# A recurrent cross-attention block with a maxout FFN: the state folded into the first layer, and the batches interleaved by hand

## The chip, the cores and the metric

The kernel runs on one core of one Trainium2 chip. A core has TensorE (PE) for matmuls, VectorE (DVE), ScalarE (ACT) and GpSimd (POOL) for elementwise work, and SyncE (SP), which here only issues transfers. Matmuls read SBUF and write PSUM, which has 8 banks of 2 KB for each of 128 partitions; DVE and ACT read PSUM. Each engine runs its own instructions in order and waits on semaphores for the others. The metric is the device time of one execution in microseconds (us).

## What is computed

There are B = 8 batches and H = 8 heads, S = 512 tokens and Ns = 32 state rows in each, D = 64 columns a head. Tokens read the state and the state reads the tokens, both by softmax attention; the heads are put side by side (8 x 64 = 512 columns), which gives 8 x (512 + 32) = 4352 rows; each row then passes a layer that takes the maximum of three products, and an output layer.

```python
def _attn_ref(x, state):
    scores = scale * np.matmul(x, state.transpose(0, 1, 3, 2))
    ...
    xread = np.matmul(a, state)
    scores2 = scale * np.matmul(state, x.transpose(0, 1, 3, 2))
    ...
    sread = np.matmul(a2, x)
    return np.concatenate([xread, sread], axis=2)

def _moe_ref(x, w1, w2, w3, w_out):
    h = np.maximum(np.maximum(x @ w1, x @ w2), x @ w3)
    return h @ w_out
```

`a` and `a2` are the softmaxes of the two score matrices. d_model is 512 and d_ff is 768. The kernel takes and gives float32 and computes in bfloat16 with float32 sums.

## The kernel before

The program has four stages, written one after the other; the Tile framework's scheduler sets the order of each engine's instructions within what the data and the buffers allow, so the end of one stage mixes with the start of the next.

*Loads.* POOL issues every load, since a transfer that converts float32 to bfloat16 is issued there: the state twice (L65, and L73 eight times into the block-diagonal `bd_sb`), x in 32 pieces (L85: one for each batch and each 128 tokens, 128 bytes a run in SBUF), then the weights w1, w2, w3 (L90) and w_out (L93).

*State.* 32 small transposes and 64 small ACT copies build `stateT_bd` (L96 to L110), the transposed state with two heads on the diagonal.

*Attention,* for each batch and each 128 tokens (L125 to L176): four transposes of x (`pxt`, helper L48) and an ACT copy `xT`; four 64-column matmuls `ps` (L143) for the scores; the exponential `e_b` on ACT (L151); row sums `den`, reciprocals `rden` and the product `a_sb` on DVE (L157 to L162); two transposes `pat` and a DVE copy `aT_b` (L176). Then for each pair of heads (L178 to L219) a 64-row matmul `pxr` (L184) multiplies a by the state, and ACT copies it into `AT` (L191); eight small matmuls `psr` (L195, L203) and three DVE operations give the state's own reads, also into `AT`.

*FFN* over `AT`, 4352 columns in nine tiles of 512 (the last has 256): for each of six blocks `m` of d_ff, three groups of four matmuls `pw` (L240) with K = 512 in four steps; ACT copies the first (L249) and DVE takes two maxima (L250, L251) into `ht`. Then for each 128 tokens six matmuls `po` (L256), an ACT copy (L264) and a transfer to HBM on SP (L265).

Of the kernel before, what the change touches and what calls it, by code (L numbers as in the profile page):

```python
# [8 lines left out]
F32 = mybir.dt.float32  # L10
BF16 = mybir.dt.bfloat16
AX = mybir.AxisListType
AF = mybir.ActivationFunctionType


@with_exitstack
def kernel(
# [9 lines left out]
):  # L27
    nc = tc.nc
# [5 lines left out]
    T = B * SP  # L34
    d_model, d_ff = moe_w1.shape
    assert HD == d_model
    assert out.shape[0] == T and out.shape[1] == d_model

    NSC = S // 128
    NKT = HD // 128  # L40
    NMT = d_ff // 128
    NKO = d_ff // 128
    NHP = H // 2

    scale = 1.0 / (D ** 0.5)

    def tr(out_ap, in_ap, ident_ap, *, start, stop, tile_position=(0, 0)):
        nc.tensor.matmul(out_ap, in_ap, ident_ap,  # L48
                         is_transpose=True, start=start, stop=stop,
                         tile_position=tile_position)  # L50

    const = ctx.enter_context(tc.tile_pool(name="const", bufs=1))
    ident = const.tile([128, 128], BF16)
    make_identity(nc, ident)
    ones128 = const.tile([128, 128], BF16)
    nc.gpsimd.memset(ones128, 1.0)

    inpool = ctx.enter_context(tc.tile_pool(name="in", bufs=1))
    atpool = ctx.enter_context(tc.tile_pool(name="at", bufs=1))
    wpool = ctx.enter_context(tc.tile_pool(name="weights", bufs=1))  # L60

    AT = atpool.tile([128, NKT, T], BF16)

    state_sb = inpool.tile([32, B, H, D], BF16)
    nc.gpsimd.dma_start(out=state_sb, in_=state.rearrange("b h n d -> n b h d"))  # L65

    bd_sb = inpool.tile([128, B, 2, 128], BF16)
    nc.gpsimd.memset(bd_sb, 0.0)
    for hq in range(2):
        for hp4 in range(4):  # L70
            h = hq * 4 + hp4
            c0 = (h % 2) * 64
            nc.gpsimd.dma_start(  # L73
                out=bd_sb[hp4 * 32:(hp4 + 1) * 32, :, hq, c0:c0 + 64],
                in_=state[:, h, :, :].rearrange("b n d -> n b d"),
            )

    stateT_bd = inpool.tile([128, B, NHP, 2 * Ns], BF16)
    nc.gpsimd.memset(stateT_bd, 0.0)

    x_sb = inpool.tile([128, B, NSC, H, D], BF16)
    xr = x.rearrange("b h (sc p) d -> p b sc h d", p=128)
    for b in range(B):
        for sc in range(NSC):
            nc.gpsimd.dma_start(out=x_sb[:, b, sc, :, :], in_=xr[:, b, sc, :, :])  # L85
# [211 lines left out]
```

## Time and profile before

| | |
|---|---|
| runs | 279.34, 281.24, 280.69 us; median 280.69 |
| span of the profiled execution, first to last instruction | 279.6 us (its own device time is not listed apart from the runs) |
| mean granted TensorE clock | 0.896 |
| loads: read from HBM | 15.73 MB |
| results: written to HBM | 8.91 MB |
| FFN stage without gaps on PE | from 101 us on |

A line of the profile's groups names the source line, the engine, the operation, what is written and read, the shape and the count; then the busy time in us, the mean of one in ns, and the time that the engine stood idle just before them with what ended it. In the chain of waits each piece is the work that released the next. The page cuts the span into 40 slices; a digit is a share in tenths, and PEclk is the clock that TensorE was granted. A piece of the timeline merges neighbouring instructions of one kind; matmuls overlap, so the time of a piece is the pitch from start to start times the count less one, and the whole duration of the last.

### The profile page before, as it was taken

To read this page: it belongs to the slowest core of one execution; us is meant where nothing else is said; L and a number is where in the kernel's file an instruction comes from. 1 tells how busy PE (TensorE), PEld (TensorE's weight loads), DVE (VectorE), ACT (ScalarE), POOL (GpSimd) and SP (SyncE) were. 2 spreads that over 40 slices of the span, in tenths; PEclk is the share of its full clock that TensorE was granted. 3 is DMA by queue.
4 is the path that set the end of the run, shared out by engine and by line. 5 is a ranking of instruction groups with operands and counts; after the bars stand their busy time and mean duration, and the time that the engine had idled before them with its cause. 6 is when DMAs were issued, how large, how long until landed. Compare 5 with 4: busy or idle time off the path is not lost.

```text
span 279.6 us, 3945 instructions
## 1 busy us (share of the span) xinstructions
PE 239.7 (86%) x1492; PEld 122.7 (44%) x1492; DVE 131.9 (47%) x332; ACT 108.2 (39%) x249; POOL 41.1 (15%) x54
## 2 busy tenths in 40 slices
PE   0128878778776699999999999999999999999993
PEld 0017546535432344444444444444444444444581
DVE  0007897777877664334235235235135145145160
ACT  0989965645553132222322331331331332322321
POOL 9999990000000000000000000000000000000000
PEclk9999995555555589999999999999999999999999
DMA  5999999910000000120120120110210210210211
GB/s 38 59 144 149 154 155 204 208 25 0 2 1 2 0 1 0 43 109 0 58 94 0 73 77 2 76 75 0 76 77 0 79 74 0 96 56 2 109 41 75
DMA packets 44801, 17.01 MB, mean 61 GB/s; under 512 B 38128, under 2 KB 40432, under 8 KB 44784
## 3 DMA queue, kind: packets, MB, share of 16 engines
q0 software_dynamic: 39888, 7.87, 33.1%
q1 hardware_dynamic: 4896, 8.92, 8.3%
q8 instruction: 11, 0.18, 0.3%
q14 instruction: 6, 0.05, 0.1%
HBM read 15.73 MB, written 8.91 MB: 88 GB/s over the span
## 4 chain that ended last, share of the span: by engine, by line
PE 77%; POOL 12%; ACT 5%; DVE 3%; DMA 1%; issue 1%; ACTq 0%; POOLq 0%
PE pw L240 48%; PE po L256 16%; POOL x_sb L85 8%; PE pxr L184 5%; ACT AT L191 3%; PE psr L195 2%; PE pxt L48 2%; POOL bd_sb L73 2%; PE psr L203 2%; DMA x_sb<-in_x_dram 1%; PE ps L143 1%; PE pat L48 1%; ACT e_b L151 1%; DVE rd L211 1%; DVE a_sb L162 1%
## 5 line engine op out<-in xcount | busy, mean ns | idle before, releaser
L240 PE MATMUL pw<-AT,w 128*128 128x512 bf16 (+1 forms) x648 | 135.7, 370 | 0.0
L240 PEld LDWEIGHTS <-w 128*128 128x128 bf16 x648 | 63.3, 98 | 69.3 <-issue 1.6
L250 DVE TENSOR_TENSOR tmpm<-tmpm,pw 128x512 f32<-128x512 f32 (+1 forms) x54 | 35.5, 657 | 96.4 <-PE pw L240 91.0
L249 ACT COPY tmpm<-pw 128x512 f32<-128x512 f32 (+1 forms) x54 | 30.3, 562 | 87.1 <-PE pw L240 87.1
L256 PE MATMUL po<-wout,ht 128*128 128x512 bf16 x204 | 45.5, 379 | 0.0
L251 DVE TENSOR_TENSOR ht<-tmpm,pw 128x512 bf16<-128x512 f32 (+1 forms) x54 | 35.5, 658 | 5.7
L264 ACT COPY o_sb<-po 128x512 f32<-128x512 f32 x34 | 19.9, 586 | 39.0 <-PE po L256 39.0
L256 PEld LDWEIGHTS <-ht 128*128 128x128 bf16 x204 | 20.0, 98 | 23.9 <-DVE ht L251 1.6
L191 ACT CAST AT<-pxr 128x512 bf16<-128x512 f32 x32 | 18.7, 585 | 29.5 <-PE pxr L184 29.5
L85 POOL DMA_DIRECT2D x_sb<-in_x_dram x32 | 28.0, 1022 | 0.0
L184 PE MATMUL pxr<-aT_b,bd_sb 64*128 64x512 bf16 x32 | 16.9, 528 | 8.6 <-ACT AT L191 8.1
L211 DVE RECIPROCAL rd<-psr 128x64 f32<-128x64 f32 x32 | 17.8, 555 | 12.7 <-PE psr L203 11.8
L157 DVE TENSOR_REDUCE den<-e_b 128x8 f32<-128x256 bf16 x32 | 12.6, 412 | 22.6 <-ACT e_b L151 22.4
L48 PE MATMUL pxt<-ident,x_sb 128*128 128x128 bf16 x128 | 19.0, 277 | 3.8 <-ACT stateT_bd L109 2.8
L139 ACT COPY xT<-pxt 128x512 bf16<-128x512 bf16 x32 | 18.2, 594 | 3.2 <-PE pxt L48 3.1
L195 PEld LDWEIGHTS <-x_sb 128*128 128x128 bf16 x128 | 8.3, 119 | 22.0 <-DVE den L157 8.9
L48 PE MATMUL pt<-ident,state_sb 32*128 32x32 bf16 x32 | 2.0, 183 | 15.4 <-ACT stateT_bd L109 9.2
L143 PE MATMUL ps<-stateT_bd,xT 128*128 128x64 bf16 x128 | 11.5, 228 | 3.9 <-ACT e_b L151 2.6
L48 PE MATMUL pat<-ident,a_sb 128*128 128x128 bf16 x64 | 12.1, 288 | 3.0 <-DVE a_sb L162 3.0
L48 PEld LDWEIGHTS <-x_sb 128*128 128x128 bf16 x128 | 11.9, 127 | 5.0 <-issue 4.9
L162 DVE TENSOR_TENSOR a_sb<-e_b,rden 128x256 bf16<-128x256 bf16 x32 | 13.4, 422 | 0.5
L195 PE MATMUL psr<-e_b,x_sb 128*128 128x64 bf16 x128 | 12.6, 229 | 1.0 <-DVE AT L216 0.9
(27 smaller groups left out, 102.2 us busy)
## 6 DMA issues: line engine op xcount, KB each, us to landing
out_dram<-o_sb SPq DMA_DIRECT2D x34, 256.0 KB, 2.0
x_sb<-in_x_dram POOLq DMA_DIRECT2D x32, 128.0 KB, 4.9
w<-in_moe_w_dram POOLq DMA_DIRECT2D x3, 768.0 KB, 12.4
wout<-in_moe_w_out_dram POOLq DMA_DIRECT2D x1, 768.0 KB, 18.7
state_sb<-in_state_dram POOLq DMA_DIRECT2D x1, 256.0 KB, 4.6
bd_sb<-in_state_dram POOLq DMA_DIRECT2D x8, 32.0 KB, 2.3
```

What stands on the lines that cost most here:

```text
L48: nc.tensor.matmul(out_ap, in_ap, ident_ap, is_transpose=True, start=start, stop=stop, tile_position=tile_position)
L85: nc.gpsimd.dma_start(out=x_sb[:, b, sc, :, :], in_=xr[:, b, sc, :, :])
L184: nc.tensor.matmul(pxr, bd_sb[p0:p0 + 64, b, hq, :], aT_b[p0:p0 + 64, hq, :, :], start=True, stop=True, tile_position=(p0, 0),)
L191: nc.scalar.copy(out=AT[:, hp, b * SP:b * SP + S], in_=pxr)
L195: nc.tensor.matmul(psr[:, 0, :], x_sb[:, b, sc, h0:h0 + 2, :], e_b[:, sc, h0:h0 + 2, :], start=(sc == 0), stop=False, tile_position=(0, 0),)
L211: nc.vector.reciprocal(out=rd, in_=psr[:, 1, :])
L240: nc.tensor.matmul(pw[i][:, :nn], w_sb[i][:, kk, m * 128:(m + 1) * 128], AT[:, kk, n0:n0 + nn], start=(kk == 0), stop=(kk == NKT - 1), til ...
L249: nc.scalar.copy(out=tmpm[:, :nn], in_=pw[0][:, :nn])
L250: nc.vector.tensor_max(tmpm2[:, :nn], tmpm[:, :nn], pw[1][:, :nn])
L251: nc.vector.tensor_max(ht[:, m, :nn], tmpm2[:, :nn], pw[2][:, :nn])
L256: nc.tensor.matmul(po, ht[:, kt, j * 128:(j + 1) * 128], wout_sb[:, kt, :], start=(kt == 0), stop=(kt == NKO - 1), tile_position=(0, 0),)
L264: nc.scalar.copy(out=o_sb, in_=po)
```

## The change

Two products that followed one another are joined. Before, a token's row was read = a @ state (`pxr`, `AT`) and then read @ w for each w. Now M = state @ w is computed for each batch, and the layer's first product is a @ M. For one batch a has 8 x 32 = 256 columns, so a `pw` group contracts over 256 in two matmuls instead of over 512 in four. M itself takes 48 units, one for each batch and each 128 columns of d_ff: eight matmuls of 384 columns (w1, w2 and w3 side by side), each on a 64-row, 32-column tile of the array at its own position, into a PSUM tile of two banks, and one copy into `M_sb`, on ACT in the loop, on ACT and DVE in turn for batches 0 and 1. The reads of the state rows keep the old form: they are collected in `AT` (256 columns) and pass all four steps of w in a ninth tile.

The attention works on half a batch or a whole one at a time. x of a batch comes in one transfer whose runs are four times as long (`p j` gives a partition four neighbouring tokens), and a copy `permute_x` brings it into the order that the matmuls read, on DVE for batch 0, on POOL for the others. The product with the reciprocals moves from DVE to POOL (L184). The state comes in float32 in eight transfers from SP and ACT and is converted on DVE. The transfers of a batch's results are two of 512 KB instead of four of 256 KB; the state rows' are eight of 64 KB.

The order is written by hand (`manual_schedule`). A start computes M for batches 0 and 1 and the attention of batch 0. The loop then has 54 slots (nine tiles of six); a slot issues two of twelve out steps of the tile before, three `pw` groups, one unit of M for the batch two ahead and one of the six attention units of the batch ahead. PSUM: four banks for `pw`, one for `po`, two for `pm`, one for the attention.

The core of the diff, added lines only (the removed ones are the kernel above):

```diff
...
+    load_w(0, 256)
+    load_x(0)
+    load_w(256, 768)
+    load_x(1)
+    nc.gpsimd.dma_start(out=wout, in_=moe_w_out.rearrange("(kk p) f -> p kk f", p=128))
+    for b in range(2, B):
...
+    def permute_x(b, eng):
+        x_nat[b] = xnp.tile([128, J, H, D], BF16, tag="xn", name="xn")
+        eng.tensor_copy(out=x_nat[b], in_=x_sb[:, b].rearrange("p h j d -> p j h d"))
...
+    def m_unit(b, m, eng):
+        pm = p_mb.tile([128, 2, 512], F32, tag="mb", name="pm")
+        for hp in range(HP):
+            for par in range(2):
+                r0 = par * 64
+                mm(pm[hp * 32:(hp + 1) * 32, par, 0:384],
+                   sbd[r0:r0 + 64, b, hp, par, :],
+                   W[r0:r0 + 64, :, hp, m * 128:(m + 1) * 128],
+                   True, True, pos=(r0, hp * 32))
+        o = M_sb[:, b, m, :, :, :].rearrange("p a i f -> p a (i f)")
+        if eng == "act":
+            nc.scalar.copy(out=o, in_=pm[:, :, 0:384])
+        else:
+            nc.vector.tensor_copy(out=o, in_=pm[:, :, 0:384])
...
+    def att_unit(b, u):
+        d = st_att.setdefault(b, {})
+        if u in (0, 1):
+            if u == 0:
+                d["xT"] = xTp.tile([128, HP, S], BF16, tag="xT", name="xT")
+            px = p_at.tile([128, 2, S], BF16, tag="at", name="px")
+            for k in range(2):
+                hp = 2 * u + k
+                for j in range(J):
+                    tr(px[:, k, j * 128:(j + 1) * 128], x_nat[b][:, j, 2 * hp:2 * hp + 2, :])
+            nc.vector.tensor_copy(out=d["xT"][:, 2 * u:2 * u + 2, :], in_=px)
+        elif u in (2, 3):
+            if u == 2:
+                d["e"] = ep.tile([128, J, 2, HP, Ns], BF16, tag="e", name="e")
+                d["a"] = ap_.tile([128, J, 2, HP, Ns], BF16, tag="a", name="a")
+            j0 = 2 * (u - 2)
+            ps = p_at.tile([128, 2, 2, HP, Ns], F32, tag="at", name="ps")
+            for jj in range(2):
+                for hp in range(HP):
+                    j = j0 + jj
+                    mm(ps[:, jj, :, hp, :], d["xT"][:, hp, j * 128:(j + 1) * 128],
+                       sbd[:, b, hp, :, :],
+                       jj == 0 and hp == 0, jj == 1 and hp == HP - 1)
+            e = d["e"][:, j0:j0 + 2]
+            ef = e.rearrange("p j a hp n -> p (j a hp) n")
+            nc.scalar.activation(out=e.rearrange("p j a hp n -> p (j a hp n)"),
+                                 in_=ps.rearrange("p j a hp n -> p (j a hp n)"),
+                                 func=AF.Exp, scale=scale)
+            den = redp.tile([128, 16], F32, tag="den", name="den")
+            nc.vector.reduce_sum(out=den, in_=ef, axis=AX.X)
+            rden = redp.tile([128, 16], BF16, tag="rden", name="rden")
+            with nc.allow_low_precision("softmax denom reciprocal"):
+                nc.vector.reciprocal(out=rden, in_=den)
+            nc.gpsimd.tensor_mul(
+                out=d["a"][:, j0:j0 + 2].rearrange("p j a hp n -> p (j a hp) n"),
+                in0=ef, in1=rden.unsqueeze(2).to_broadcast((128, 16, Ns)))
+        elif u == 4:
+            e = d["e"]
+            pr = p_at.tile([128, 512], F32, tag="at", name="pr")
...
+            for hp in range(HP):
+                for j in range(J):
+                    mm(psr[:, hp, :, :], x_nat[b][:, j, 2 * hp:2 * hp + 2, :],
+                       e[:, j, :, hp, :], hp == 0 and j == 0, False)
+            for par in range(2):
+                for j in range(J):
+                    mm(pd, ones_h[:, par, :],
+                       e[:, j, par, :, :], False, par == 1 and j == J - 1)
...
+            nc.vector.reciprocal(out=rd, in_=pd.rearrange("p (hp n) -> p hp n", hp=HP))
...
+        else:
+            d["aT"] = aTp.tile([128, 2, S], BF16, tag="aT", name="aT")
+            pa = p_at.tile([128, 2, S], BF16, tag="at", name="pa")
+            for par in range(2):
+                for j in range(J):
+                    tr(pa[:, par, j * 128:(j + 1) * 128], d["a"][:, j, par, :, :])
+            nc.vector.tensor_copy(out=d["aT"], in_=pa)
...
+    def up(g, m, i, first_of_tile):
...
+        pw = p_up.tile([128, S], F32, tag="pw", name="pw")
+        if g < B:
+            for par in range(2):
+                mm(pw, M_sb[:, g, m, par, i, :], st_att[g]["aT"][:, par, :],
+                   par == 0, par == 1)
+        else:
+            for hp in range(HP):
+                mm(pw[:, :nn], W[:, i, hp, m * 128:(m + 1) * 128], AT[:, hp, :],
+                   hp == 0, hp == HP - 1)
+        if i == 0:
+            t = tmpp.tile([128, S], BF16, tag="t0", name="t0")
+            nc.scalar.copy(out=t[:, :nn], in_=pw[:, :nn])
+        elif i == 1:
+            t = tmpp.tile([128, S], BF16, tag="t1", name="t1")
+            nc.vector.tensor_max(t[:, :nn], hts[g, "t"][:, :nn], pw[:, :nn])
+        else:
+            t = None
+            nc.vector.tensor_max(hts[g][:, m, :nn], hts[g, "t"][:, :nn], pw[:, :nn])
+        hts[g, "t"] = t
...
+    def out_step(g, step):
+        j, part = divmod(step, 3)
+        if part == 0:
+            outs["po"] = p_o.tile([128, d_model], F32, tag="po", name="po")
+        for kt in (2 * part, 2 * part + 1):
+            mm(outs["po"], hts[g][:, kt, j * 128:(j + 1) * 128], wout[:, kt, :],
+               kt == 0, kt == MT - 1)
+        if part == 2:
+            if j % 2 == 0:
+                outs["o"] = op.tile([128, 2, d_model], F32, tag="o", name="o")
+            o = outs["o"]
+            nc.scalar.copy(out=o[:, j % 2, :], in_=outs["po"])
...
+    for m in range(2):
+        m_unit(0, m, "act")
+        m_unit(1, m, "dve")
+    permute_x(0, nc.vector)
+    for u in range(4):
+        att_unit(0, u)
+    permute_x(1, nc.gpsimd)
+    for m in range(2, MT):
+        m_unit(0, m, "act")
+        m_unit(1, m, "dve")
+        if m == 2:
+            att_unit(0, 4)
+        if m == 4:
+            att_unit(0, 5)
+            att_unit(1, 0)
+    att_q = [(b, u) for b in range(1, B) for u in range(6)][1:]
+    m_q = [(b, m) for b in range(2, B) for m in range(MT)]
+    slots = [(g, m) for g in range(B + 1) for m in range(MT)]
+    for k, (g, m) in enumerate(slots):
+        if g > 0:
+            out_step(g - 1, 2 * m)
+        up(g, m, 0, m == 0)
+        up(g, m, 1, False)
+        if g > 0:
+            out_step(g - 1, 2 * m + 1)
+        up(g, m, 2, False)
+        if m_q:
+            m_unit(*m_q.pop(0), "act")
+        if att_q:
+            if att_q[0][1] == 3 and att_q[0][0] + 1 < B:
+                permute_x(att_q[0][0] + 1, nc.gpsimd)
+            att_unit(*att_q.pop(0))
+    for step in range(6):
+        out_step(B, step)
...
```

What this does to the order shows at three places. On PE, in the middle of the program: before, in the dense FFN stage, a `pw` group of one weight, the next with its wait, and the first out step of the tile (`pw` and `po` are the PSUM tiles of the two layers, `w` and `M_sb` weights, `ht` the maxima; rows that only repeat are left out).

```order
L240 LDWEIGHTS w_124
L240 MATMUL pw_2137<-AT,w_124 128x512
L240 LDWEIGHTS w_126
L240 MATMUL pw_2138<-AT,w_126 128x512 [waits DVE_49]
L256 LDWEIGHTS ht
L256 MATMUL po<-wout,ht 128x512
```

And now, in a slot of the loop (`pm` is M's PSUM tile, `sbd` the block-diagonal state, `xn` the permuted x, `px` its transposes):

```order
L117 LDWEIGHTS ht
L117 MATMUL po<-wout,ht 128x512
L117 LDWEIGHTS M_sb
L117 MATMUL pw<-aT,M_sb 128x512 [waits DVE_49]
L117 LDWEIGHTS sbd
L117 MATMUL pm<-W,sbd 32x384 [waits Activation_49]
L120 LDWEIGHTS xn
L120 MATMUL px<-ident,xn 128x128 [waits DVE_49]
```

Between two groups of the FFN there now stand a unit of M, which waits for ACT's copy of the unit before, and a unit of attention, which waits for DVE's copy of the one before.

On DVE, in the middle of the attention before, where the softmax's operations of one batch and the state's reads follow one another:

```order
L157 TENSOR_REDUCE den<-e_b 128x8 [waits Activation_49]
L211 RECIPROCAL rd<-psr 128x64 [waits PE_49]
L176 COPY aT_b<-pat 128x2x128 [waits PE_49]
L160 RECIPROCAL rden<-den 128x8 [waits DVE_49]
L212 TENSOR_TENSOR AT<-psr,rd 64x32 [waits DVE_49]
L162 TENSOR_TENSOR a_sb<-e_b,rden 128x256 [waits DVE_49]
```

And now, in the loop, where the two maxima of each slot (`t` and `ht`) alternate with an attention unit's operations:

```order
L240 TENSOR_TENSOR ht<-t_635,pw 128x512 [waits DVE_49,PE_49]
L161 COPY xT<-px 128x1024 [waits PE_49]
L237 TENSOR_TENSOR t_675<-t_670,pw 128x512 [waits PE_49,Activation_49]
L240 TENSOR_TENSOR ht<-t_675,pw 128x512 [waits DVE_49,PE_49]
L180 TENSOR_REDUCE den<-e 128x16 [waits Activation_49]
L183 RECIPROCAL rden<-den 128x16 [waits DVE_49,Pool_49]
L237 TENSOR_TENSOR t_721<-t_716,pw 128x512 [waits PE_49,Activation_49]
```

The product `a_sb` has left DVE, and the maxima of a slot stand behind the reduce of the slot before, which waits for ACT's exponential.

On POOL, at the start of the program before, the loads of the state and of x:

```order
L65 DMA state_sb<-in_state_dram 32x64x64
L68 MEMSET bd_sb 128x2048
L79 MEMSET stateT_bd 128x2048
L73 DMA bd_sb<-in_state_dram 32x8x64 [waits Pool_49]
L85 DMA x_sb<-in_x_dram 128x8x64 [waits DMASW1_49]
```

And now, where the first weights lead, and the products and permutations of the loop follow behind the last load:

```order
L82 DMA W<-in_moe_w_dram 128x4x256 x3
L85 DMA x_sb<-in_x_dram 128x8x256
L82 DMA W<-in_moe_w_dram 128x4x512 x3
L93 DMA wout<-in_moe_w_out_dram 128x6x512 [waits DMASW0_49]
L85 DMA x_sb<-in_x_dram 128x8x256 [waits DMASW6_49]
L184 TENSOR_TENSOR a<-e,rden 128x512 [waits DVE_49,Activation_49] x2
L112 COPY xn<-x_sb 128x2048 [waits DMASW7_49]
```

The weights have moved ahead of x, the memsets are gone from this queue, and a load with a wait holds what stands behind it.

286 lines of the change are left out of this document (84 added, 202 removed).

## The prediction

> **What bounds the kernel now.** I read the page first (busy times, slices, chain), then the chain in order of time, then the stretches, and last single rows for prices. From the page:
>
> ```profile
> span 279.6 us, 3945 instructions
> PE 239.7 (86%) x1492; PEld 122.7 (44%) x1492; DVE 131.9 (47%) x332; ACT 108.2 (39%) x249; POOL 41.1 (15%) x54
> PEclk9999995555555589999999999999999999999999
> PE 77%; POOL 12%; ACT 5%; DVE 3%; DMA 1%; issue 1%; ACTq 0%; POOLq 0%
> ```
>
> TensorE carries 77% of the chain. In order of time the chain falls into a stage of loads and attention, and from 95 us on a stage in which PE never stops. Its last pieces (start, duration, what):
>
> ```profile
> 244.15 15.54 PE pw L240 x72
> 259.69 5.18 PE po L256 x24
> 264.87 7.86 PE pw L240 x72
> 272.73 2.60 PE po L256 x12
> 275.36 0.58 ACT o_sb L264
> ```
>
> 72 matmuls of 512 columns take 15.54 us: 0.216 us each; so do those of the output layer (5.18/24), and 256 columns take 0.109 (7.86/72). The stretches (us, then busy time of PE, PEld, DVE, ACT, POOL; granted clock; DMA; GB/s):
>
> ```profile
> 24.00:34.00 10.00, 8.68 (x116) 6.32 (x114) 8.66 (x34) 9.09 (x21) 10.00 (x12) 1.00 2.36 151
> 37.00:42.00 5.00, 3.27 (x34) 1.50 (x32) 4.51 (x18) 3.00 (x7) 4.78 (x6) 0.96 2.19 157
> 48.00:50.00 2.00, 1.83 (x12) 0.67 (x12) 1.43 (x6) 0.72 (x2) 0.00 (x0) 0.50 1.16 209
> 50.00:80.00 30.00, 23.29 (x216) 14.53 (x216) 22.75 (x85) 16.52 (x36) 0.00 (x0) 0.50 0.27 47
> 104.00:264.00 160.00, 160.00 (x743) 72.50 (x742) 64.13 (x94) 44.89 (x77) 0.00 (x0) 1.00 0.13 49
> ```
>
> So the second half is bound by PE alone, at full clock with no gap, while DVE is 40% busy. The first 95 us are loads, then short dependent steps at half clock. The change attacks both: fewer matmul columns in layer one, and the attention put into the dense stage.
>
> **PE prices.** Single rows of the timeline (start, duration of the piece):
>
> ```profile
> 20.21 1.01 PE L48 MATMUL pxt<-ident,x_sb 128*128 128x128 bf16 x8 [2.81 <-ACT stateT_bd L109]
> ...
> 35.63 0.74 PE L48 MATMUL pxt<-ident,x_sb 128*128 128x128 bf16 x8
> 36.25 0.28 PE L48 MATMUL pat<-ident,a_sb 128*128 128x128 bf16 x2
> 36.48 0.28 PE L195 MATMUL psr<-e_b,x_sb 128*128 128x64 bf16 x4
> 36.59 0.28 PE L203 MATMUL psr<-e_b,ones 128*128 128x64 bf16 x4
> ...
> 51.02 0.40 PE L195 MATMUL psr<-e_b,x_sb 128*128 128x64 bf16 x4
> 51.22 0.40 PE L203 MATMUL psr<-e_b,ones 128*128 128x64 bf16 x4
> ...
> 97.94 1.47 PE L240 MATMUL pw<-AT,w 128*128 128x512 bf16 x3
> ...
> 100.33 0.22 PE L203 MATMUL psr<-e_b,ones 128*128 128x64 bf16 x2
> 100.51 0.37 PE L184 MATMUL pxr<-aT_b,bd_sb 64*128 64x512 bf16 x1
> 100.82 0.23 PE L203 MATMUL psr<-e_b,ones 128*128 128x64 bf16 x2
> ```
>
> From start to start: a transpose takes 0.077 us at full clock ((36.25-35.63)/8) and about 0.103 at half ((1.01-0.29)/7 with the last one's 0.29); a 64-column matmul 0.028 (0.11/4) and 0.05 (0.20/4); 512 columns 0.216 and 0.43 (97.94: three in 1.47 with 0.6 for the last). The 64-row matmul between two 128-row ones starts 0.12 us after the first pair has streamed and holds the next for 0.31, of which 0.216 is its own stream: each change of array shape costs about 0.1. The first row also corrects the clock row of the page: it reads 9 from the start, but at 20 us the transposes still go at the half-clock pitch; the full clock came later, in the busy stretch from 24 us.
>
> **Layer one.** A pw group falls from four 512-column matmuls to two, for 48 of 54 groups of three; the state rows keep four of 256. Per batch: up 36 x 0.216 = 7.77, out 24 x 0.216 = 5.18, together 12.95 us in six slots of 2.16. The first batch has no out steps beside it: 1.30 a slot.
>
> **The fold, M.** 48 units of eight 384-column matmuls on 64 x 32 tiles; 36 lie in the loop. No row shows two matmuls in the array at once, so I bound: all eight together, two shape changes 0.2, eight issues at 0.028, one stream of 384/512 x 0.216 = 0.16, makes 0.59; one after the other makes 0.2 + 8 x 0.162 = 1.5. I take 0.7, near the low end: the eight use disjoint array tiles, and each pair of row halves writes its own bank. At half clock the same sums give 0.92 and 2.76; I take 1.0.
>
> **Attention on PE.** Per batch 24 transposes (1.85), 32 matmuls of 64 columns (0.9), 8 of 128 (0.55): 3.3 us, 0.55 a slot. The 64-row xread matmuls with their waits are gone.
>
> **The other engines.** Prices by shape (busy, mean ns | idle before):
>
> ```profile
> L251 DVE TENSOR_TENSOR ht<-tmpm,pw 128x512 bf16<-128x512 f32 x48 | 33.0, 687 | 5.0
> L249 ACT COPY tmpm<-pw 128x512 f32<-128x512 f32 x48 | 28.1, 585 | 82.5 <-PE pw L240 82.5
> L211 DVE RECIPROCAL rd<-psr 128x64 f32<-128x64 f32 x32 | 17.8, 555 | 12.7 <-PE psr L203 11.8
> L157 DVE TENSOR_REDUCE den<-e_b 128x8 f32<-128x256 bf16 x32 | 12.6, 412 | 22.6 <-ACT e_b L151 22.4
> L151 ACT ACTIVATE e_b<-ps 128x256 bf16<-128x256 f32 x32 | 11.6, 390 | 1.5 <-PE ps L143 1.5
> L176 DVE COPY aT_b<-pat 128x256 bf16<-128x256 bf16 x32 | 8.0, 249 | 2.6 <-PE pat L48 2.2 <-PE ps L143 0.3
> L216 DVE TENSOR_TENSOR AT<-psr,rd 64x32 bf16<-64x32 f32 x32 | 6.2, 194 | 0.6
> L160 DVE RECIPROCAL rden<-den 128x8 bf16<-128x8 f32 x32 | 4.9, 173 | 0.3
> L251 DVE TENSOR_TENSOR ht<-tmpm,pw 128x256 bf16<-128x256 f32 x6 | 2.5, 421 | 0.6
> L249 ACT COPY tmpm<-pw 128x256 f32<-128x256 f32 x6 | 2.2, 373 | 4.6 <-PE pw L240 4.6
> L79 POOL MEMSET stateT_bd<- 128x2048 bf16 x1 | 1.8, 1828 | 0.0
> ```
>
> A DVE column costs 1.04 ns ((687-421)/256), an ACT column 0.83. So a 768-column M eviction takes 0.80 on ACT, 0.95 on DVE; a 512-column exp 0.60; the reduce 0.68; the 128-column reciprocal about 1.0 (6.8 ns a column between 8 and 64); a 16-column one 0.23; each AT product 0.29. The 1024-column bf16 copy lies between 0.54 (0.15 fixed, the rest of 249 scaled) and 1.0 (249 x 4); I take 0.65. DVE per batch: 12 x 0.687 + 3 x 0.65 + 2 x 0.91 + 1.0 + 0.58 = 13.6, or 2.27 a slot; ACT: 0.59 + 0.80 + 0.39 + 0.20 = 1.98. Both stay under PE's 2.16 + 0.55 + 0.7 = 3.41, so I cost them at nothing in the loop. That cover is thin in one place: the reduce waits on DVE for the exp, which stands behind the M eviction on ACT, and the next slot's two maxima queue behind it. From M's end this is 0.80 + 0.60 + 0.68 + 0.23 + 0.69 + 0.69 = 3.7 us, more than a slot; the four pw buffers lend about one more slot. The copy of po has the 0.86 us of two pw groups to hide its 0.59. On POOL two products and a permutation per batch: 0.46 and 1.83 us at the memset's rate, an estimate of 1.2 and 2.5 since they read as well; they have two slots (6.8 us) before the transposes of a.
>
> **The start.** Loads (transfers, to landing):
>
> ```profile
> DMA to landing us min/median/max: 9.4/12.4/15.4
> L265 SPq DMA_DIRECT2D out_dram<-o_sb x34: 332/333/531, 116.6 to 276.0; - x34
> ```
>
> The first of these rows is that of the three weight loads: 768 KB every 3.75 us or so, the 209 GB/s of the stretch at 48 us. The first third of the weight columns is 768 KB behind three issues on POOL from 1.5 us: all there at about 9.5 (8 to 12). The state comes in eight loads from SP and ACT, 0.33 an issue, at about 5; its cast, eight transposes and two copies take some 2.5 more (by DVE's and ACT's columns) and end before the weights are there. The remaining two thirds land by 21, before they are used. POOL issues 15 loads in place of 45; its first product stands behind all of them, and the last load waits for the second part of w3 to land, near 20 us. The product is wanted at 24 and read at 37, so this queue costs nothing; if the loads ran at the 151 GB/s of the stretch at 24 us in place of 209, it would be free at 26 and still cost nothing. From 9.5 PE is cold. M units share one PSUM tile, so each costs its matmuls, an eviction and two hand-offs: 1.0 + 0.88 + 0.2 = 2.1. Four of them: 17.9. Permuting x on DVE 1.2 (2048 columns, 0.9 to 2.0): 19.1. Attention units 0 to 3 share one tile too: 2 x (0.82 + 0.2 + 0.65 + 0.1) + 2 x (0.4 + 0.2 + 0.6 + 0.1), without the last exp: 5.5, so 24.6. Eight more M units with units 4, 5 and the next 0 between them, partly under the evictions: 17.4. The loop starts at 42 (34 to 50).
>
> **The sum.** 42.0; first batch 6 x 2.55 = 15.3 and 2.0 until the clock has risen; five batches 30 x 3.41 = 102.3; the seventh 12.95 + 5 x 0.55 = 15.7; the eighth 12.95; state rows 7.86 + 5.18 = 13.0; last out steps 2.6; the end 4.3 (275.3 to 279.6) and three more issues on SP at 0.333: 5.3. Span 211.2. The profiled span is 279.6 and the runs' median 280.69, so I add 1.1: 212.
>
> **Rivals.** *Two at a time.* The weights of a tile might wait until its row half is free: M then costs 0.2 + 4 x 0.162 + issue = 0.9 at full clock and 1.6 at half: 36 x 0.2 + 12 x 0.6 = 14 more, 226. No row speaks against it. The Trainium skill, "TensorE: Matmul & The Clock Gate", part on packing small matmuls, has this rule: a weight load overlaps a running matmul only where the row group differs. By it this rival is the case; the same section's measured packings of column tiles speak for more overlap, and no run here shows either.
>
> *No packing.* M at 1.5 and 2.76: 36 x 0.8 + 12 x 1.76 = 50 more, 262. PEld and PE overlap in every stretch, so loads at least run beside matmuls.
>
> *A chain instead of PE.* The exp to maxima chain above, or the single attention tile, sets the slots: 0.5 us on each of 36 is 18, so 230. Speaking for it: one buffer each for po, pm and the attention; against it: a slot of slack in most waits.
>
> *The clock stays at half* (slower). The stretches show half clock with PE 78% busy, and the fall comes near 42 us after a stretch that was 65% busy. At half clock a slot is 4.27 + 0.84 + 1.0 = 6.1, the loop about 300, the time 345; it decides for slower once more than half of the loop ((280.7-212)/(345-212) = 52%) runs so. Against it: in the 10 us from 24 us, 87% busy, the clock rose, and my loop leaves PE hardly a gap. The Trainium skill, same page, part on the clock gate, lets the clock fall only after a whole idle window of some 3.4 us; by that this rival has no chance. The trace differs: its clock fell while PE worked 3.27 of 5 us, so I keep one.
>
> **Chances.** Forecast 212 (198 to 221): 0.47. Two at a time: 0.20. Chain: 0.13. No packing: 0.10. Clock: 0.03. Shorter than 198, by a start of 34 us and M at 0.59: 0.07. The range 196 to 240 leaves out no packing, the clock and a little below: 2 in 10. About 1% is what a measurement of this kernel can tell from no change. Faster by more than that holds in all cases but the clock's: 0.97; within 1% 0.01; slower 0.02.
>
> **What would show it.** pw groups of two matmuls 0.43 apart; an M unit's eight starts 0.03 apart (together), in pairs, or 0.16 apart; slots of 3.4 us at 1.00; the loop's first pw matmul near 42 us; the last PE instruction near 206. I am wrong if PE idles before pm or pw for DVE or ACT in the loop, if the clock row shows 5 past 60 us, or if the loop starts after 50.

## The result and the profile after

The changed kernel takes 196.97 us (median of 4 runs, 195.98 to 197.42), against 280.97 us (median of 4) for the kernel before on the same chip: a ratio of 0.7006, 95% interval 0.6974 to 0.7038. The forecast was 212 with a range from 196 to 240, so the direction and the range held, the range by 1 us at its low end, and one of the four runs lies under it. These are the lines of the page after that answer to those of before (engines; PE and its clock in 40 slices; the chain by engine and by line):

```profile
span 194.2 us, 3652 instructions
...
PE 164.0 (84%) x1468; PEld 83.2 (43%) x1468; DVE 121.0 (62%) x201; ACT 91.6 (47%) x148; POOL 42.6 (22%) x44
...
PE   0134564799799999999999999999999999999980
...
PEclk9999999999999999999999999999999999999999
...
PE 82%; ACT 6%; DVE 5%; DMA 3%; issue 1%; ACTq 1%; DVEq 0%
PE pw L117 35%; PE po L117 23%; PE pm L117 8%; PE px L120 5%; PE pr L117 5%; PE ps L117 3%; DMA st<-in_state_dram 3%; ACT M_sb L144 2%; ACT o L256 2%; DVE M_sb L146 2%; PE pa L120 2%; DVE xT L161 1%; ACTq L69 1%; ACT e L176 1%; PE pst L120 1%
```

PE did 239.7 us of work before and does 164.0 now. It still carries the chain, but it is dense from the ninth slice on (39 us; only the eleventh has a gap) instead of from 95 us. The stretches say the same (us, then busy time of PE, PEld, DVE, ACT, POOL; clock; DMA share; GB/s):

```profile
60.00:160.00 100.00, 99.75 (x925) 49.31 (x924) 75.54 (x126) 59.37 (x96) 21.49 (x17) 1.00 0.15 62
```

DVE has risen to three quarters of its time in there, and PE has still no gap to speak of. One slot of the loop in the timeline, from one M unit to the next (start, duration of the piece, what):

```profile
84.80 0.35 PE L117 MATMUL pm<-W,sbd 64*32 64x384 bf16 x8
85.09 0.62 PE L120 MATMUL pa<-ident,a 128*128 128x128 bf16 x8
85.55 0.59 PE L117 MATMUL po<-wout,ht 128*128 128x512 bf16 x2
85.98 1.03 PE L117 MATMUL pw<-aT,M_sb 128*128 128x512 bf16 x4
86.84 0.59 PE L117 MATMUL po<-wout,ht 128*128 128x512 bf16 x2
87.28 0.59 PE L117 MATMUL pw<-aT,M_sb 128*128 128x512 bf16 x2
87.80 0.36 PE L117 MATMUL pm<-W,sbd 64*32 64x384 bf16 x8
```

The slot is 3.00 us (87.80 - 84.80). A pair of 512-column matmuls starts 0.43 after the one before, as forecast. The M unit keeps PE for 0.29 from its first start (85.09 - 84.80), and about 0.1 goes by between the last 512-column stream and that start (87.80 - 87.28 - 0.43): 0.39 in all, where the sum had 0.7. Eight transposes take 0.46 to the next instruction, 0.057 each, where the sum had 0.077.

The start, in the chain in order of time:

```profile
2.19 5.62 DMA st<-in_state_dram
...
12.23 0.81 ACT M_sb L144
...
13.08 0.57 PE pm L117 x8
...
13.67 0.97 DVE M_sb L146
...
14.68 0.56 PE pm L117 x8
```

The state, not the weights, is waited for first. Then the matmuls of an M unit and its eviction follow strictly one after the other: 1.60 us from 13.08 to 14.68, and 1.4 to 1.5 where ACT evicts. The loop's first pw matmul starts at 37.03. The first three still run at half clock, though the page's clock row reads 9 from the first slice:

```profile
37.03 1.46 PE L117 MATMUL pw<-aT,M_sb 128*128 128x512 bf16 x3
```

With 0.6 for the last one, (1.46 - 0.6) / 2 is 0.43 a matmul, twice 0.216. So the page's row does not show the clock there, and the pitch of the matmuls is what to read.

### The profile page after: what moved, and what is told of

The parts are those of the page before. It is cut to its first block, busy times and chain, and to the rows that moved or that the text cites. A ratio compares the mean times of both kernels' runs of the same rounds, so it can differ in the third digit from the quotient of the medians.

```text
span 194.2 us, 3652 instructions
## 1 busy us (share of the span) xinstructions
PE 164.0 (84%) x1468; PEld 83.2 (43%) x1468; DVE 121.0 (62%) x201; ACT 91.6 (47%) x148; POOL 42.6 (22%) x44
## 4 chain that ended last, share of the span: by engine, by line
PE 82%; ACT 6%; DVE 5%; DMA 3%; issue 1%; ACTq 1%; DVEq 0%
PE pw L117 35%; PE po L117 23%; PE pm L117 8%; PE px L120 5%; PE pr L117 5%; PE ps L117 3%; DMA st<-in_state_dram 3%; ACT M_sb L144 2%; ACT o L256 2%; DVE M_sb L146 2%; PE pa L120 2%; DVE xT L161 1%; ACTq L69 1%; ACT e L176 1%; PE pst L120 1%
## 5 line engine op out<-in xcount | busy, mean ns | idle before, releaser
L117 PE MATMUL pw<-aT,M_sb 128*128 128x512 bf16 x288 | 78.2, 384 | 0.0
L144 ACT CAST M_sb<-pm 128x768 bf16<-128x768 f32 x42 | 33.6, 799 | 37.8 <-PE pm L117 37.7
L237 DVE TENSOR_TENSOR t<-t,pw 128x512 bf16<-128x512 bf16 (+1 forms) x54 | 34.8, 644 | 25.9 <-ACT t L234 20.5
L117 PEld LDWEIGHTS <-M_sb 128*128 128x128 bf16 x288 | 28.0, 99 | 33.6 <-issue 1.6
L234 ACT CAST t<-pw 128x512 bf16<-128x512 f32 (+1 forms) x54 | 30.5, 565 | 23.7 <-PE pw L117 23.6
L240 DVE TENSOR_TENSOR ht<-t,pw 128x512 bf16<-128x512 bf16 (+1 forms) x54 | 35.5, 658 | 7.3 <-PE pw L117 2.3
L184 POOL TENSOR_TENSOR a<-e,rden 128x512 bf16<-128x512 bf16 x16 | 16.7, 1043 | 101.8 <-DVE rden L183 101.8
L256 ACT COPY o<-po 128x512 f32<-128x512 f32 x34 | 19.9, 586 | 20.4 <-PE po L117 20.2
L117 PE MATMUL pm<-W,sbd 64*32 64x384 bf16 x384 | 19.6, 374 | 9.0 <-ACT M_sb L144 5.5
L85 POOL DMA_DIRECT2D x_sb<-in_x_dram x8 | 7.1, 888 | 7.5 <-DMA W<-in_moe_w_dram 5.8
```

The source lines that it names most:

```text
L117: nc.tensor.matmul(out_ap, lhsT, rhs, start=start, stop=stop, tile_position=pos)
L144: nc.scalar.copy(out=o, in_=pm[:, :, 0:384])
L184: nc.gpsimd.tensor_mul(out=d["a"][:, j0:j0 + 2].rearrange("p j a hp n -> p (j a hp) n"), in0=ef, in1=rden.unsqueeze(2).to_broadcast((128, ...
L234: nc.scalar.copy(out=t[:, :nn], in_=pw[:, :nn])
L237: nc.vector.tensor_max(t[:, :nn], hts[g, "t"][:, :nn], pw[:, :nn])
L240: nc.vector.tensor_max(hts[g][:, m, :nn], hts[g, "t"][:, :nn], pw[:, :nn])
```

## The experiments

Ten kernels were run, each against the kernel before; the edits are against the changed kernel unless another is named.

**Fold or interleaving?** Two kernels keep one half of the change each. Both keep the new loads, the larger attention units and the product on POOL; what these are worth was not measured apart. The first goes on interleaving, and takes the fold back: four matmuls per pw group, with the read of the state in two units a batch.

```diff
-                mm(pw, M_sb[:, g, m, par, i, :], st_att[g]["aT"][:, par, :],
+                mm(pw, W[:, i, hp, m * 128:(m + 1) * 128], st_att[g]["R"][:, hp, :],
...
-        if m_q:
-            m_unit(*m_q.pop(0), "act")
+        if m >= 4 and g + 1 < B:
+            read_unit(g + 1, m - 4)
```

> The interleaved order kept, the fold undone: each batch's token rows are read again as a @ state (two units of four 32-row matmuls of 512 columns and a 1024-column ACT copy), and a pw group has four matmuls. Theory (the time is PE's columns, the two parts add): start to the first pw matmul 26 us in place of 37 (no M), a slot of a middle batch 4.07 (24.4 a batch in place of 18.0), time about 236 us. Rival 1 (the order gives nearly all of the gain, M costs what the fold saves): 200 to 210. Rival 2 (the fold gives nearly all, the order little): 260 or more.

Measured: 239.08 us (238.22 to 239.57), ratio to before 0.8534 (0.8492 to 0.8576). The stretch of 100 us in its loop:

```profile
60.00:160.00 100.00, 99.32 (x684) 50.20 (x694) 56.55 (x92) 36.42 (x57) 15.66 (x12) 1.00 0.12 48
```

and its first pw matmul in the timeline:

```profile
28.83 3.48 PE L117 MATMUL pw<-R,W 128*128 128x512 bf16 x11 [0.22 <-issue]
```

PE is as dense as with the fold. So the fold is worth 42.1 us on top of the interleaving (239.08 - 196.97). Its sum: 288 matmuls fewer at 0.216 are 62.2, the 36 M units in the loop cost 36 x 0.39 = 14.0, and the start is 8.2 longer (37.03 - 28.83): 40.0. The 14 read units that are gone from the loop took some 0.43 each by the pitch in its timeline, another 6.0, which makes 46.0. Of the 4 too many, 2 are waits that the loop has only with the fold (1.19 ahead of `pa`, and 1.9 instead of 1.2 at the po tile); the rest is not accounted for.

The second keeps the fold and takes the interleaving away: M and attention of all batches come first, then the dense stage.

```diff
+    for b in range(B):
+        engs = ["act", "dve"] * 3
+        for u in range(6):
+            ...
+            m_unit(b, u, engs[u])
+            att_unit(b, u)
```

To make room for eight batches of `aT`, two other pools have one buffer fewer; PE waits for neither.

> The fold kept, the interleaving undone: M and the attention of all eight batches first (a unit of each in turn, the same tiles and single buffers), then all up and out steps. Theory: the first stage takes the unit chains' time, 12 to 13 us a batch on top of 11, so the dense stage starts near 110 us, at half clock before it and at full clock from some 4 us after its start; it takes 119 us; time about 231 us. Rival 1 (the first stage is short, most of the gain was the fold and the loads): 205 or less. Rival 2 (without dense matmuls beside them the chains are slower than in the start of the changed kernel): 250 or more.

Measured: 247.24 us (246.89 to 247.38), ratio 0.8827 (0.8789 to 0.8865): between the theory's 231 and the 250 of rival 2. The dense stage starts at 118.26 us instead of 110 and takes 126.8 (to 245.1) instead of 119, of which 4.5 are waits at the single po tile. The stretch of the first stage:

```profile
60.00:118.00 58.00, 39.82 (x504) 27.51 (x506) 37.17 (x61) 15.90 (x23) 15.91 (x13) 1.00 0.01 1
```

and one batch of it in the timeline:

```profile
87.51 0.52 PE L117 MATMUL pm<-W,sbd 64*32 64x384 bf16 x8 [1.31 <-DVE M_sb L146]
87.96 1.04 PE L117 MATMUL pr<-e,xn 128*128 128x64 bf16 x16
...
89.78 0.52 PE L117 MATMUL pm<-W,sbd 64*32 64x384 bf16 x8
91.62 1.01 PE L120 MATMUL pa<-ident,a 128*128 128x128 bf16 x8 [1.31 <-DVE AT L204]
...
100.21 0.52 PE L117 MATMUL pm<-W,sbd 64*32 64x384 bf16 x8 [1.31 <-DVE M_sb L146]
```

A batch takes 12.70 us (100.21 - 87.51). In it PE waits 3.8 for copies out of a single tile (1.31 twice, the rest in waits of 0.2 to 0.3), and otherwise works at half the pace (0.52 for an M unit, 1.01 for eight transposes, against 0.36 and 0.62 in the loop), though it is busy 69% of the stretch and the clock row reads 1.00. Its longest stretch of unbroken work here is 2.8 us, from 87.51 to 90.3. On top of the fold, then, interleaving is worth 50 us (247.24 - 196.97): it hides the waits, and it keeps PE at full clock. How the 50 us divide between the two was not measured.

**Do the eight matmuls of M run together?** This was the term with the widest bounds. All eight are put on one place of the array, 64 rows by 128 columns, with the same count of columns streamed; M holds other values in this kernel.

```diff
-                mm(pm[hp * 32:(hp + 1) * 32, par, 0:384],
-                   sbd[r0:r0 + 64, b, hp, par, :],
-                   W[r0:r0 + 64, :, hp, m * 128:(m + 1) * 128],
-                   True, True, pos=(r0, hp * 32))
+                mm(pm[:, par, 0:384], sbd[0:64, b, 0:2, :, :],
+                   W[0:64, :, hp, m * 128:(m + 1) * 128],
+                   True, True, pos=(0, 0))
```

> All eight matmuls of an M unit go to one array tile (64 rows, 128 columns, position 0, 0), so none can run beside another; M holds other values, the copies stay. Theory (the eight run together in the changed kernel, 0.39 us a unit in the loop): a unit costs 8 x 0.162 + 0.2 = 1.5 us at full clock, 1.1 more on each of 36, and at half clock 2.8 in place of 0.55 on each of 12 in the start, so 250 us (240 to 262). Rival (the eight were already one behind another or in pairs, or issue and shape changes make their time): 197 to 215.

Measured: 263.06 us (one run). The unit in its loop:

```profile
74.25 1.47 PE L117 MATMUL pm<-W,sbd 64*128 64x384 bf16 x8
75.66 0.41 PE L117 MATMUL ps<-sbd,xT 128*128 128x64 bf16 x8
```

1.41 from its start to the next one, against 0.29: 1.12 more on each of 36 units are 40 us, and the 12 units of the start, at half clock, take 2.7 instead of 0.52 each: 26 more. Together 66, and the time rose by 66. So the eight do run together in the changed kernel, and this is about what the forecast's rival without packing would have cost, which put it at 50.

The order in which the tiles are written was turned round, the halves of the rows outside:

```diff
-        for hp in range(HP):
-            for par in range(2):
+        for par in range(2):
+            for hp in range(HP):
```

> The same eight tiles of an M unit in another order: the four column tiles of the upper row half first, then the four of the lower half, in place of alternating halves. Theory (a tile's weight load waits for no matmul of another tile): no change, 197 us within 1%. Rival (the Trainium skill, TensorE: Matmul & The Clock Gate, part on packing small matmuls: a weight load overlaps a running matmul only where the row group differs): the four of one half follow one another, a unit costs about 0.2 + 7 x 0.162 = 1.3, 0.9 more on each of 36, 230 us or more.

Measured: 196.43 us (195.89 to 196.74), ratio 0.7008 (0.6971 to 0.7045), no change; an M unit is a piece of 0.35 to 0.36 as before, and one of its matmuls alone lasts 0.333, so all eight start within 0.03. Four column tiles of one row half follow one another here, and they overlap just as well. The Trainium skill, "TensorE: Matmul & The Clock Gate", part on packing small matmuls, lets a weight load overlap a running matmul only where the row group differs; these runs do not bear that out.

At last each unit's matmuls in the loop are issued twice:

```diff
+        for _ in range(2 if b >= 2 else 1):
             for hp in range(HP):
                 for par in range(2):
```

> The eight matmuls of each unit of M in the loop are issued twice, 36 units. Theory A (PE sets the loop, and the eight run together at the pace of issue, 0.025 each, so that a second set adds 0.20): 36 x 0.20 = 7 us, 204 (203 to 206). Theory B (a set costs its whole piece again, 0.36): 13 us, 210 (208 to 212). Rival (the slot is set by the evictions and maxima, and PE has slack): 196 to 199.

Measured: 202.14 us (201.57 to 203.60), 5.2 more. The unit:

```profile
83.24 0.52 PE L117 MATMUL pm<-W,sbd 64*32 64x384 bf16 x16
83.69 0.64 PE L117 MATMUL pr<-e,xn 128*128 128x64 bf16 x16
```

The piece grows from 0.36 to 0.52, by 0.16, and 36 x 0.16 is 5.8. That is below both expectations, and it is one stream of 384 columns (384/512 x 0.216 = 0.16). The 0.16 would also fit eight issues of 0.020, so the starts decide. The matmuls of the unit that are under way in each stretch (length, busy time and count, then clock, DMA share, GB/s):

```profile
83.24:83.27 0.03, 0.03 (x8) 1.00 0.00 0
83.27:83.41 0.14, 0.14 (x8) 1.00 0.00 0
83.41:83.44 0.03, 0.03 (x16) 1.00 0.00 0
```

The first eight start within 0.03, none starts for 0.14, then the second eight start within 0.03. So a set of eight costs one stream, neither eight issues nor its whole piece again. The other 0.23 of the unit's 0.39 was not paid a second time. The time follows PE's work, so PE is the bound of the loop.

**What sets the start?** The first of these kernels has M one batch ahead of its use instead of two, so that six units go from the start into the slots of the first batch:

```diff
-    for m in range(2):
-        m_unit(0, m, "act")
-        m_unit(1, m, "dve")
+    m_unit(0, 0, "act")
+    m_unit(0, 1, "dve")
...
-    m_q = [(b, m) for b in range(2, B) for m in range(MT)]
+    m_q = [(b, m) for b in range(1, B) for m in range(MT)]
```

> M of batch 1 moves out of the start into the slots of batch 0, so that M runs one batch ahead instead of two. Theory (a unit of M costs 1.45 to 1.6 us in the start, where each waits for the eviction of the unit before, and 0.39 in the loop, where PE is the limit): six units leave the start, 8.5 us; six come into the loop, 6 x 0.39 = 2.3 us. First pw matmul at 28.5, time 191 (189 to 193). Rival (the start is set by the attention chain of the first batch and by the loads, and its M units lie beside them): the first pw matmul stays above 34, and the added units make the time 196 to 199.

Measured: 190.36 us (188.95 to 191.43), ratio 0.6780 (0.6744 to 0.6815). The theory held: the first pw matmul is 7.3 us earlier (8.5 were forecast), as its row shows.

```profile
29.70 2.34 PE L117 MATMUL pw<-aT,M_sb 128*128 128x512 bf16 x5 [0.34 <-issue]
```

The second leaves the twelve units where they were, but puts each into two of the four pw tiles, evicted half by ACT and half by DVE:

```diff
+    def m_unit_halves(b, m):
+        for par, eng in ((0, "act"), (1, "dve")):
+            pw = p_up.tile([128, S], F32, tag="pw", name="pw")
+            ...
...
-        m_unit(0, m, "act")
-        m_unit(1, m, "dve")
+        m_unit_halves(0, m)
+        m_unit_halves(1, m)
```

> Only the start: each unit of M there goes into two of the four pw tiles, and ACT and DVE evict one half each, so that the next unit's matmuls run beside. Theory (the hand-off of the single tile is what a unit in the start costs): a unit falls from 1.45 to about 0.6 (0.52 of matmuls at half clock, or 0.55 for 384 columns on DVE); the second part of the weights at 20 and the first batch's attention then limit the start; first pw matmul at 29, time 189 (187 to 192). Rival (chain of attention and loads): first pw above 34, 195 to 197.

Measured: 189.45 us (187.97 to 189.73), ratio 0.6740 (0.6706 to 0.6774), first pw matmul at 30.05. The first four units in the timeline:

```profile
10.83 0.51 PE L117 MATMUL pw<-W,sbd 64*32 64x384 bf16 x4 [1.09 <-ACT sbd L129]
11.56 0.87 PE L117 MATMUL pw<-W,sbd 64*32 64x384 bf16 x16 [0.22 <-DVE sbd L130]
12.73 0.97 PE L117 MATMUL pw<-W,sbd 64*32 64x384 bf16 x12 [0.30 <-DVE M_sb L161]
```

They are done by 13.7, where one tile had its fourth start at 16.12. So the eviction and the hand-off of the single PSUM tile were what a unit in the start cost, and not its matmuls. The edit adds tiles and halves each copy at once; which of the two gives more was not measured.

**All together, and a surprise.** The two are joined. At the end of the program the state rows' last six out steps go into pw tiles, so that they need not wait for the single po tile, and two transfers replace eight:

```diff
-                for q in range(4):
-                    bb = 4 * j + q
-                    nc.sync.dma_start(out=out[bb * SP + S:(bb + 1) * SP, :],
-                                      in_=o[q * 32:(q + 1) * 32, j % 2, :])
+                rows = out.rearrange("(b r) f -> b r f", b=B)[4 * j:4 * j + 4, S:, :]
+                nc.sync.dma_start(out=rows, in_=o[:, j % 2, :])
```

> M one batch ahead, halves in the start, and at the end the state rows' outputs in pw tiles (no wait for the single po tile) with two DMAs in place of eight. Theory: start: M of the first batch in 2.4 us less hand-offs, then bound by loads (20) and the first batch's attention; first pw at 25 (-12); 2.3 back in the slots; -0.7 -0.2 at the tile, and six issues of about 0.48 fewer behind the last copy, of which 1.5 lie on the end: 197 - 12 + 2.3 - 2.4 = 185 (182 to 188). Rival (parts overlap): no better than the better of the two alone, 188 to 191.

Measured: 192.46 us (191.28 to 192.95), ratio 0.6853 (0.6819 to 0.6886): worse than either part alone. The loop starts earlier than in both (28.31) and PE ends at 181.7, so the loss is behind it. The last rows of its timeline:

```profile
181.12 1.79 SPq L283 DMA_DIRECT2D out_dram<-o  x2
181.75 0.58 ACT L274 COPY o<-pw 128x512 f32<-128x512 f32 x1 [0.67 <-PE pw L117]
```

and a stretch behind them (the column before the last is the busy share of the 16 DMA engines):

```profile
184.00:186.00 2.00, 0.00 (x0) 0.00 (x0) 0.00 (x0) 0.00 (x0) 0.00 (x0) 0.94 0.25 83
```

The span runs on for 8.8 us after the last copy (182.33 to 191.1), with a DMA share of 0.25, as of four engines of sixteen. In that time nearly all of both transfers still moves (0.52 MB from 182.4 on), not the last one alone. The outermost dimension of each, the batch, has size 4. To test that, the eight transfers are put back, the last four issued by SP and ACT in turn:

```diff
-                rows = out.rearrange("(b r) f -> b r f", b=B)[4 * j:4 * j + 4, S:, :]
-                nc.sync.dma_start(out=rows, in_=o[:, j % 2, :])
+                for q in range(4):
+                    bb = 4 * j + q
+                    eng = nc.scalar if j == 1 and q % 2 else nc.sync
+                    eng.dma_start(out=out[bb * SP + S:(bb + 1) * SP, :],
+                                  in_=o[q * 32:(q + 1) * 32, j % 2, :])
```

> As e8, but the state rows go out again in eight transfers of 64 KB, the last four of them issued by SP and ACT in turn. Theory (the single transfer of 256 KB for four batches was slow by itself: its copy ended at 182.33, the span at 191.1, 8.8 us, where the kernel after the change ends 3.9 us after its last copy): the end falls to 182.33 + 2 x 0.48 + 0.33 + 1.7 = 185.3, the time to 187 (185 to 188.5). Rival (the PSUM tiles or the order made the end late, not the transfer): 191 to 193.

Measured: 187.37 us (187.05 to 188.06), ratio 0.6684 (0.6656 to 0.6712). The last copy ends at 181.52 and the span at 185.3, 3.8 later, and the DMA share there is 0.63:

```profile
181.00:183.00 2.00, 0.00 (x0) 0.00 (x0) 0.00 (x0) 0.51 (x1) 0.00 (x0) 1.00 0.63 165
```

So the transfers' form was the loss. That ACT issues two of them now is not the reason: with all eight on SP the changed kernel ends 3.9 us after its last copy. The Trainium skill, "DMA: Bandwidth & Descriptors", part on how many engines a transfer uses, has the rule: the count is the largest number up to 16 that divides the slowest dimension that is not 1, on both sides; 4 here, and the trace agrees with its 0.25.

**The clock of the start.** To that kernel matmuls of zeros are added that nobody reads, 20 ahead of the first transposes and 3 to 6 in the gaps behind:

```diff
+    def warm(n):
+        pz = p_o.tile([128, 512], F32, tag="po", name="pz")
+        for _ in range(n):
+            nc.tensor.matmul(pz, zero[:, 0:128], zero, start=True, stop=True,
+                             tile_position=(0, 0))
```

> As e9, with 45 or so matmuls of zeros by 512 columns, read by nobody: 20 ahead of the first transposes, then groups of 3 to 6 in the gaps of the start. Theory (half clock in the start is for want of work on PE before; kept at work it rises within some 4 us and stays): the start's PE pieces shrink (two groups of transposes 2 x 0.45, ps 2 x 0.2, pr and ones 0.9, two more groups of transposes 0.9) 3.1 us, the first slots 1.1: 183 (181.5 to 185). Rival A (the clock falls back in the pauses, which stay longer than the fillers): the fillers cost 0 to 3 us, 187 to 190. Rival B (the start is bound by the loads, so full clock gives only what comes behind the second part of the weights at 20.6): 185 to 186.5.

Measured: 184.81 us (184.52 to 185.27), ratio to before 0.6587 (0.6560 to 0.6614): 12.2 us under the changed kernel and the fastest of this study. Its start:

```profile
1.19 6.69 PE L71 MATMUL pz<-zero 128*128 128x512 bf16 x20 [1.19 <-DVE zero L66]
8.52 0.62 PE L129 MATMUL pst<-ident,st 128*128 128x128 bf16 x8 [0.64 <-DVE st L134]
...
17.59 0.39 PE L126 MATMUL ps<-sbd,xT 128*128 128x64 bf16 x8
20.72 0.35 PE L126 MATMUL pw<-W,sbd 64*32 64x384 bf16 x8 [2.73 <-DMA W<-in_moe_w_dram]
...
26.53 1.47 PE L126 MATMUL pw<-aT,M_sb 128*128 128x512 bf16 x6
```

Twenty matmuls would take 8.5 us at half the pace; 6.69 means that some ten of them, about 4.4 us, went by before the clock rose. From there on the pieces shown go at full pace, across a pause of 2.73 us too. Most of the time that the attention won is lost again at 20.72, where PE waits for the second part of the weights, which is rival B; the loop still starts 1.4 us earlier than without the fillers (26.53 against 27.92), and its first six pw matmuls take 1.47 instead of 2.60. Together 2.5, and the time fell by 2.56. The time lies in the theory's range (181.5 to 185) and just under that of rival B, and both hold in part.

## Why the prediction was right, point by point

- *What bounds the kernel.* Right. PE works 99.75 of 100 us in the loop, and the doubled units show that the time follows PE's work.
- *Layer one.* Right: 0.43 from pair to pair, half the matmuls; with its costs taken off, the fold is worth 42 us on top of the interleaving.
- *The fold, M.* The mechanism was right, the size was off: "I take 0.7 ... I take 1.0" at half clock. It is 0.39 in the loop, and a piece of 0.52 at half clock. The lower bound of 0.59 was itself too high, because it gave each of the eight an issue of 0.028, the pitch of 64-column matmuls on the whole array. The doubled units showed one stream of 0.16 and some 0.23 for all the rest. The starts that the prediction asked for, 0.03 apart, came all eight within 0.03.
- *Attention on PE.* Mis-sized as well: 0.46 a slot, not 0.55. The transposes were priced at 0.077 from a row of before that holds a gap of 0.19 behind its fourth; those four alone take 0.39 there, 0.056 each with 0.22 for the last. Eight in the loop go at 0.057.
- *The slots.* 30 of them take 90.13 us (52.49 to 142.62), 3.00 each, not 3.41. M gives 30 x 0.31 = 9.3 of the difference of 12.2 and the attention 30 x 0.09 = 2.7: both terms together explain it.
- *The other engines.* They cost nothing in the 30 full slots, as the sum had it. The thin place was the one that the prediction named: DVE waits 20.5 us for `t` from ACT, without PE waiting for DVE. The copy of po has two pw groups to hide behind only every second time; the other times it has one, 0.43 for its 0.59, and where no M unit stands in the slot PE waits (0.24, five times from 158 us on). The groups (busy, mean ns | idle before) have ACT's M eviction at 0.80 as priced, POOL's product at 1.04 for an estimated 1.2 and its permutation at 1.89 for 2.5:

```profile
L144 ACT CAST M_sb<-pm 128x768 bf16<-128x768 f32 x42 | 33.6, 799 | 37.8 <-PE pm L117 37.7
...
L237 DVE TENSOR_TENSOR t<-t,pw 128x512 bf16<-128x512 bf16 (+1 forms) x54 | 34.8, 644 | 25.9 <-ACT t L234 20.5
...
L184 POOL TENSOR_TENSOR a<-e,rden 128x512 bf16<-128x512 bf16 x16 | 16.7, 1043 | 101.8 <-DVE rden L183 101.8
...
L112 POOL COPY xn<-x_sb 128x2048 bf16<-128x2048 bf16 x7 | 13.2, 1891 | 0.0
```

- *The start.* 37.03 instead of 42, from two errors of opposite sign. "They end before the weights are there" failed: the state landed at 7.8, not 5, and the first M matmul waited for it until 10.92, 1.4 late. But a unit cost 1.45 to 1.60 instead of 2.1, since its matmuls at half clock take 0.52 and not 1.0: the first four came 1.65 cheaper, the other eight with the attention units between them 4.1 (23.73 to 37.03, for 17.4). The permutation on DVE took 0.68 instead of 1.2. The four attention units took 5.4 (18.33 to 23.73), as forecast 5.5. The splitting into halves showed that eviction and hand-offs set a unit there, as the prediction's sum had it.
- *The end.* 1.0 too low for the last out steps: a single po tile makes their six matmuls wait for ACT's copy, which the sum did not have, since no pw group stands between them. Behind PE's last matmul the span took 4.6 instead of 5.3. The rows of the timeline:

```profile
186.01 1.45 PE L117 MATMUL po<-wout,ht 128*128 128x512 bf16 x6 [0.24 <-ACT o L256]
...
187.54 0.59 ACT L256 COPY o<-po 128x512 f32<-128x512 f32 x1 [1.59 <-PE po L117]
188.16 3.86 SPq L266 DMA_DIRECT2D out_dram<-o  x8
188.18 1.46 PE L117 MATMUL po<-wout,ht 128*128 128x512 bf16 x6 [0.72 <-ACT o L256]
```

- *The sum.* 11.2 for M (36 x 0.31), 3.7 for the attention (41 slots x 0.09) and 5.0 for the start come off 211.2, and 1.0 is added at the end: 192.3, against a span of 194.2. The 2 us left are, as far as is known, the wait of the first batch (1.19 ahead of `pa`) and the five waits of 0.24 at the single po tile, less the 0.7 at the end.
- *The rivals.* Two at a time, no packing and a chain are refuted by the runs on the tiles' order, on one tile, and by the doubled units and the dense loop. The clock at half did not come in the loop. It was there in the start, where the sum had it, and all through the first stage of the kernel without interleaving. The case that came true is close to the one given 0.07, with M below 0.59 and a start of 37: the bounds were worked out with a floor that was no floor. That 196.97 still lies above 196 is luck: M, the attention and the start were all priced too high, 19.9 us together, and only waits of 1 to 3 us went the other way.

## What to carry to other kernels

Where a chain of small dependent steps stands ahead of a dense stage, spread it over the dense stage's slots: the chain is hidden, and TensorE keeps its clock; this was worth more here (50 us) than a fold that halves a layer's matmuls (42 us), each on top of the other. Price a group of matmuls on disjoint tiles of the array as one stream plus a fixed entry (0.16 and 0.23 here, the one shape tried), not as so many issues. Ahead of the dense stage count the evictions and PSUM hand-offs rather than the matmuls, and give them more tiles; and leave no small dimension (here 4) outermost in a transfer on which the end waits.

## What the runs showed of the hardware that was not expected

- Eight matmuls of 64 rows x 32 columns by 384 take 0.36 us as a piece in either order of the tiles, all eight started within 0.03; a second set of eight adds 0.16.
- With two transfers of 256 KB whose outermost dimension is 4, the DMA share stood at 0.25, as of four engines of 16, and the program ended 8.8 us after the last copy; with eight of 64 KB in their place, 3.8.
- TensorE rose to full clock after some 4.4 us of unbroken 512-column matmuls, and stayed there over a pause of 2.73 us. The Trainium skill, "TensorE: Matmul & The Clock Gate", part on the clock gate, lets it rise after a window of some 3.4 us of sustained work and fall after as long an idle one; that rise and that pause agree. Three other runs show that the busy time of the profile does not decide it. Without interleaving the clock did not rise in 58 us at 69% busy. With M on one place of the array PE worked from 35.73 to 42.94 without a wait, most of it on 64-row matmuls, and at the end of these 7.2 us a unit still took 2.74, the half pace:

```profile
40.20 2.74 PE L117 MATMUL pm<-W,sbd 64*128 64x384 bf16 x8
```

And in the start of the kernel with halves the clock had risen and fell again, between two groups of eight transposes, with no wait of PE above 0.78 us:

```profile
26.61 0.62 PE L120 MATMUL pa<-ident,a 128*128 128x128 bf16 x8
28.02 1.01 PE L120 MATMUL px<-ident,xn 128*128 128x128 bf16 x8 [0.78 <-DVE aT L228]
```

The fall in the kernel before, near 42 us with no wait of PE above 0.7 us, is of this kind. What decides there stays open: no run was made on it.
- The clock row of the page reads full in the start of the program, where the pitch of the matmuls is that of half clock.
